# One 512-column first product for two token pairs, and a rewritten order of steps, in a gated-loop attention and feed-forward kernel

## The chip, the cores and the metric

One Trainium2 chip, one core of it. The time is the device time of one execution in microseconds, and the median of several executions is compared. TensorE (PE in the rows) does matrix products into PSUM, VectorE (DVE) and ScalarE (ACT) do elementwise work, GpSimd (POOL) and SyncE (SP) mostly issue DMA transfers.

## The reference

A gated linear attention with a complex decay for 4 batches, 8 heads, 768 steps and a head size of 48, then a feed-forward block with a silu:

```python
def _attn_ref(q, k, v, a_re, a_im):
    mag = np.sqrt(a_re * a_re + a_im * a_im)
    scale = np.minimum(mag, 0.999) / (mag + 1e-06)
    a_re_n, a_im_n = (a_re * scale, a_im * scale)
    for t in range(S):
        ar, ai = (a_re_n[:, :, t, :, None], a_im_n[:, :, t, :, None])
        new_re = ar * S_re - ai * S_im
        new_im = ar * S_im + ai * S_re
        kv = np.einsum('bhd,bhe->bhde', k[:, :, t], v[:, :, t])
        S_re, S_im = (new_re + kv, new_im)
        y[:, :, t] = np.einsum('bhd,bhde->bhe', q[:, :, t], S_re)

def _moe_ref(x, w_in, w_out):          # x: 3072 x 384, d_ff = 2048
    h = x @ w_in
    g = h * (1.0 / (1.0 + np.exp(-h)))
    return (g @ w_out).astype(np.float32)
```

## The kernel before

The 3072 tokens are 24 chunks n of 128; two chunks make a pair p, of which there are 12. Chunks 0 to 3 are the first of the four batches, chunk n carries on from chunk n - 4. For each chunk the attention runs in matrix form: gates and angles of a pair (steps G0 to Ga, ScalarE and VectorE), running sums of the angle and of the log decay by a triangular matmul (phase, L), rounding and sine (rd, turn, trig), decays (exp), decayed and rotated keys and queries (dk, dq, K, Q, or rk, rq), their transposes, scores (w) and their mask (m), the output (y), its copy into the pair's xT (x, and xd for the part of two heads that travels by DMA), and the state for the chunk four later (s, ss, sd, S).

The feed-forward part takes a pair's 256 tokens as moving operand of the first product, 256 hidden units at a time: step h:p.jp, jp from 0 to 7, fills one PSUM bank with two blocks of 128 units by 256 tokens. For pairs 2 to 11 the fp32 product is made of three products in fp32r: x and the weights are each split in forms, xH (head), xL (tail) and xD (difference) for x, the weights' head, `fine1` and `mixed1` on the other side (`hidden`, L749, and `sums`, L764). The forms of x are made by xh (ScalarE, L778), xt and xg (VectorE). Then silu (g:p.jp, ScalarE), the three forms of its result (gr on ScalarE, gb and gc on VectorE), and the second product r:p.jp (`result_of_parts`, L939), which adds 3 forms x 2 blocks of units x 2 output tiles to the pair's two PSUM tiles. After jp = 7 the tiles are copied out and stored (oc).

From pair 2 on, two neighbouring pairs make a quad; they share the loads of the weights' `fine` part and `diff` part from DRAM (lv, lw) and the `mixed` tile (vx), which are made under the quad's first pair (`lead`). The PSUM tiles are two banks for attention, two for h and four for the output. The buffers of xH, xL and xD are one for even and one for odd pairs; before pair 2 the same buffers serve the start of the attention.

The order of every engine's work is one list of 1899 steps written out by hand (L1079 to L1218). Each engine runs its own instructions in the order of that list, and so do the DMA queues: a step with g behind its number loads over GpSimd's queue, other loads and the weight blocks (F) go over SyncE's. H, J and R convert weight blocks, `warm:n` issues n matmuls without use, `hold` takes one weight buffer until GpSimd gets there. ScalarE loads a table of functions when a step needs a function of another set (`special`, L309).

Of the kernel before, what the change touches and what calls it, by code (L numbers as in the profile page):

```python
# [70 lines left out]
def kernel(  # L71
# [703 lines left out]

    def x_head(p):
        t = A[p]["xH"] = moe.tile([C, ND, T], F32R, tag=f"xH{p % 2}", name=f"xH{p}", bufs=1)
        nc.scalar.mul(t, A[p]["xT"], MORE * SPLIT / FINER)  # L778
# [616 lines left out]
```

## Time and profile before

| | us |
|---|---|
| median of 3 runs | 616.13 |
| lowest, highest | 613.35, 617.29 |
| the profiled execution | 616.33 |
| its span, first to last instruction | 614.5 |

The rows below are from the profiled execution; their times count from the start of the span. Matmuls overlap in the rows: the time of one runs from its start until its last result is in PSUM, so the distance of two starts, not the time of one, tells what a matmul costs in a sequence.

### The profile page before, as it was taken

How to read it: one execution, taken by the hardware profiler on the slowest of the kernel's cores; microseconds unless marked ns; L12 is line 12 of the kernel's file. 1: busy time of each engine (PE TensorE's matmuls, PEld its weight loads, DVE VectorE, ACT ScalarE, POOL GpSimd, SP SyncE). 2: the span in 40 equal slices, each digit the busy share in tenths (PEclk: the TensorE clock that was granted, in tenths of full speed). 3: DMA queues.
4: the chain of work that ended last, by engine and by line, in shares of the span. 5: the costliest groups of instructions: out<-in, count | busy, mean ns of one | idle time of the engine just before them, and what ended most of it. 6: DMA issues, size and time to landing. Idle time of an engine off the chain costs nothing. (4 is left out here: it accounts for less than half of the span.)

```text
span 614.5 us, 12718 instructions
## 1 busy us (share of the span) xinstructions
PE 584.0 (95%) x4404; PEld 538.2 (88%) x4404; DVE 495.9 (81%) x765; ACT 434.0 (71%) x689; POOL 222.4 (36%) x389
## 2 busy tenths in 40 slices
PE   3678999999998999999999999999999999999997
PEld 2457877777768999999999999999999999999996
DVE  5689989889988899888798989889989686566453
ACT  7789989799496798598797596897984742333222
POOL 6256343543631345533272553325640233000000
PEclk9879999999999999999999999999999999999999
DMA  9859698987778989768967768786768576664462
GB/s 180 201 136 190 184 195 189 203 160 205 202 234 244 218 163 238 161 157 186 212 159 186 154 156 225 180 187 149 177 156 255 146 186 155 203 201 136 160 201 80
DMA packets 167733, 112.30 MB, mean 183 GB/s; under 512 B 137725, under 2 KB 143425, under 8 KB 167665
## 3 DMA queue, kind: packets, MB, share of 16 engines
q1 hardware_dynamic: 151920, 89.69, 57.0%
q0 software_dynamic: 12288, 17.23, 14.0%
q10 hardware_dynamic: 3456, 4.52, 2.0%
q8 instruction: 36, 0.59, 0.4%
q14 instruction: 33, 0.26, 0.1%
HBM read 81.14 MB, written 11.47 MB: 151 GB/s over the span
## 5 line engine op out<-in xcount | busy, mean ns | idle before, releaser
L596 POOL DMA_DIRECT2D T<-sq x120 | 69.9, 590 | 67.3 <-PE h L768 24.0
L914 ACT ACTIVATE head<-g 128x512 fp32r<-128x512 f32 x75 | 47.4, 632 | 56.1 <-PE o L953 47.1
L312 ACT ACTIVATE g<-h 128x512 f32<-128x512 f32 x96 | 56.2, 593 | 40.5 <-PE h L768 34.4
L768 PE MATMUL h<-xL,fine 128*128 128x256 f32 x480 | 83.7, 283 | 0.8 <-DMA fine<-w_firsts 0.8
L768 PE MATMUL h<-xD,mixed 128*128 128x256 f32 x480 | 82.8, 280 | 1.0 <-DVE mixed L862 0.6
L306 ACT ACT_TABLE_LOAD x63 | 80.8, 1283 | 2.3 <-ACT ot L966 0.8
L858 DVE SCALAR_TENSOR_TENSOR tail<-g,head 128x512 fp32r<-128x512 f32 x75 | 51.5, 687 | 31.3 <-ACT head L914 21.6
L527 POOL DMA_DIRECT2D dec<-ends x48 | 31.3, 663 | 106.7 <-DMA ends<-eq 99.2
L768 PEld LDWEIGHTS h<-xD,mixed 128*128 128x128 f32 x480 | 68.5, 189 | 1.6 <-DVE mixed L862 1.0
L768 PEld LDWEIGHTS h<-xL,fine 128*128 128x128 f32 x480 | 68.3, 188 | 1.1 <-DMA fine<-w_firsts 1.1
L953 PE MATMUL o<-coarse,head 128*128 128x384 f32 x300 | 66.8, 344 | 0.0
L953 PE MATMUL o<-diff,gd 128*128 128x384 f32 x300 | 65.4, 339 | 0.7 <-DMA diff<-w_diffs 0.7
L768 PE MATMUL h<-xH,firsts 128*128 128x256 f32 x360 | 62.5, 282 | 0.0
L609 PE MATMUL a<-T 96*128 96x128 f32 x384 | 52.8, 285 | 3.9 <-ACT T L601 3.9
L953 PE MATMUL o<-fine,tail 128*128 128x384 f32 x260 | 55.6, 336 | 0.0
L609 PEld LDWEIGHTS a<-T 96*128 96x128 f32 x384 | 49.9, 198 | 6.5 <-ACT T L601 4.9
L953 PEld LDWEIGHTS o<-diff,gd 128*128 128x128 f32 x300 | 53.6, 188 | 1.5 <-DVE w L620 1.0
L862 DVE TENSOR_TENSOR gd<-tail,g 128x512 fp32r<-128x512 f32 x75 | 51.4, 686 | 4.2 <-PE o L953 0.2
L768 PEld LDWEIGHTS h<-xH,firsts 128*128 128x128 f32 x360 | 52.7, 188 | 0.5 <-issue 0.4
L953 PEld LDWEIGHTS o<-coarse,head 128*128 128x128 f32 x300 | 50.2, 188 | 1.5 <-issue 1.3
L728 POOL DMA_DIRECT2D S<-ssq x84 | 46.9, 607 | 12.8 <-DVE ssq L717 6.7
L953 PEld LDWEIGHTS o<-fine,tail 128*128 128x128 f32 x260 | 46.2, 188 | 0.0
(159 smaller groups left out, 1283.8 us busy)
## 6 DMA issues: line engine op xcount, KB each, us to landing
fine<-w_firsts SPq DMA_DIRECT2D x40, 384.0 KB
diff<-w_diffs SPq DMA_DIRECT2D x40, 384.0 KB
T<-sq SPq DMA_DIRECT2D x120, 64.0 KB
T<-sq POOLq DMA_DIRECT2D x120, 64.0 KB, 3.8
small<-in_moe_w_in_dram SPq DMA_DIRECT2D x16, 384.0 KB
raw<-in_moe_w_out_dram SPq DMA_DIRECT2D x16, 384.0 KB
small<-in_moe_w_out_dram SPq DMA_DIRECT2D x16, 384.0 KB
raw<-in_moe_w_in_dram SPq DMA_DIRECT2D x24, 192.0 KB
```

The costliest lines, as they stand in the source:

```text
L306: nc.scalar.preload_act_table_set(SETS[of][0])
L312: nc.scalar.activation(out=out, in_=in_, func=func, **kw)
L527: nc.gpsimd.dma_start(out=x["dec"][a * D:(a + 1) * D], in_=ends[n].rearrange("(h d) -> d h", d=D))
L596: (nc.gpsimd if a % 2 else nc.sync).dma_start(out=to[ts(b, Q), :, a], in_=X[n]["sq"][ts(a, Q), b].rearrange("p w h x -> p (w h) x"))
L609: nc.tensor.matmul(ps[:, h], lhsT=x["kT"][hh * HH + h], rhs=x["qT"][hh * HH + h], start=True, stop=True)
L728: (nc.gpsimd if g % 2 else nc.sync).dma_start(out=to[ts(b, Q), r, :, e], in_=sq[ts(g, Q), :, b, 0:e.stop - e.start])
L768: nc.tensor.matmul(ps[:, ji], lhsT=w(dc, ji), rhs=x[:, dc], start=(f == 0 and dc == 0), stop=(f == len(forms) - 1 and dc == ND - 1))
L858: nc.vector.scalar_tensor_tensor(out=dst, in0=whole, scalar=MORE / FINER, in1=head.bitcast(F32), op0=ALU.mult, op1=ALU.subtract)
L862: nc.vector.tensor_tensor(out=dst, in0=tail, in1=whole, op=ALU.subtract)
L914: nc.scalar.mul(g_form(p, jp, "head"), A[p]["g", jp], MORE * SPLIT / FINER)
L953: nc.tensor.matmul(to, lhsT=left[:, ji, ts(m, C)], rhs=right(ji), start=(first_ and ji == 0 and n == 0), stop=(last_ and ji == 1 and n == 2))
```

## The change

For the pairs 2 to 9 (`wide`), the four quads, a step h:p.jp computes one block of 128 units, block 2 jp + p % 2, for the 512 tokens of both pairs, as 9 matmuls of 512 columns in place of 18 of 256. So the two pairs' xH are the halves of one tile, and so are xL and xD (`quad_tile`), for all pairs; before pair 2 the halves of those tiles serve the start (`spare_form`). The second product of a step then has one block of units and the tokens of both pairs: 3 forms x 2 pairs x 2 output tiles, with the first and last step counted over the 16 steps of a quad. Pairs 0 and 1 (fp32) and 10 and 11 keep their products. The list of steps holds the same 1899 steps in another order from beginning to end.

```diff
@@ hidden(p, jp)
             fine, diff = (A[lead(p)][name, jp] for name in ("fine1", "mixed1"))
+            if wide(p):
+                forms = [(J[kind, lead(p)], w) for kind, w in
+                         (("xH", head_of(lead(p), jp)), ("xL", fine), ("xD", diff))]
+                for f, (x, w) in enumerate(forms):
+                    for dc in range(ND):
+                        nc.tensor.matmul(ps, lhsT=w[:, dc, ts(p % 2, C)], rhs=x[:, :, dc],
+                                         start=(f == 0 and dc == 0),
+                                         stop=(f == len(forms) - 1 and dc == ND - 1))
+                return
...
+    def wide(p):
+        return QUADS <= p < NP - 2
+
+    def quad_tile(key, i, dtype, name):
+        both = J.setdefault(key, None)
+        if both is None:
+            both = J[key] = moe.tile([C, 2, ND, T], dtype, tag=key[0], name=name, bufs=1)
+        return both[:, i]
+
+    def x_form(p, kind):
+        return quad_tile((kind, p - p % 2), p % 2, F32R, f"{kind}{p}")
+
+    def spare_form(kind, i, name):
+        return quad_tile((kind, -1), i, F32, name).rearrange("p c x -> p (c x)")
+
     def x_head(p):
-        t = A[p]["xH"] = moe.tile([C, ND, T], F32R, tag=f"xH{p % 2}", name=f"xH{p}", bufs=1)
+        t = A[p]["xH"] = x_form(p, "xH")
...
     def result(p, jp):
+        if wide(p):
+            result_of_quads(p, jp)
+            return
...
+    def result_of_quads(p, jp):
+        x, both = A[p], (lead(p), lead(p) + 1)
+        for q_ in both:
+            if "o" not in A[q_]:
+                A[q_]["o"] = o_tiles(q_, 2)
+        y = A[both[0]]
+        y["through"] = y.get("through", 0) + 1
+        first_, last_ = y["through"] == 1, y["through"] == NJ
+        forms = ((x["head", jp], W["coarse"][:, jp * 2 + p % 2]),
+                 (x["tail", jp], W["fine", jp][:, p % 2]),
+                 (x["gd", jp], y["diff", jp][:, p % 2]))
+        for n, (left, right) in enumerate(forms):
+            for i, q_ in enumerate(both):
+                for m in range(2):
+                    nc.tensor.matmul(A[q_]["o"][m].rearrange("p n c -> p (n c)"),
+                                     lhsT=left[:, i, ts(m, C)], rhs=right,
+                                     start=(first_ and n == 0), stop=(last_ and n == 2))
```

The order, at the start, and where the first quad (pairs 2 and 3) hands over to the second (4 and 5) and that to the third (6 and 7):

```diff
-                re:0 im:0 e0:0 re:1g e1:0 e2:0 q:0g e3:0 im:2g im:1 e4:0 e0:1 hold: e1:1 re:2g e6:0
-                e2:1 im:3g re:3g e5:0 k:0g F: v:0g e7:0 e4:1 e8:0 e6:1 F: L:0 e3:1 exp:0 e7:1 e8:1
-                at:0.0 warm:30 e5:1 F: dk:0 G0:1 k:1g an:0.0 dq:0 G5:1 phase:0 rd:0 R: turn:0
-                warm:34 at:0.1 sm:1 trig:0 L:1 an:0.1 H: rk:0.0 G1:1 rk:0.1 rq:0.0 phase:1 rd:1 H:
...
+                re:0 im:0 hold: e0:0 warm:34 re:1g e1:0 re:2g e2:0 e4:0 e0:1 e3:0 im:1 k:0g F: e5:0
+                e6:0 e1:1 im:2g warm:30 e7:0 L:0 e2:1 e4:1 e3:1 e8:0 e5:1 exp:0 re:3g e6:1 e7:1 H:
+                at:0.0 e8:1 an:0.0 at:0.1 an:0.1 warm:20 phase:0 im:3g G0:1 rd:0 dk:0 turn:0 F:
+                q:0g R: G8:1 q:1g v:0g R: ends:0 trig:0 G5:1 L:1 rk:0.0 sm:1 J: G1:1 dq:0 rq:0.0
+                exp:1 rk:0.1 s:0 F: H: rq:0.1 G7:1 lk:1 F: k:1g phase:1 dq:1 G2:1 rd:1 G4:1 sm:0 H:
+                H: v:1g lk:0 thirds:0 J: G3:1 last:0 L:2 R: R: G6:1 exp:2 t:0.0 F: turn:1 G9:1 dk:1
+                q:2g trig:1 T:0.0 S:0 t:0.2 T:0.2 L:3 re:4g Ga:1 k:2g t:0.1 ends:1 exp:3 F: t:0.3
+                rk:1.0 rq:1.1 rk:1.1 phase:2 rd:2 t:1.0 T:0.1 t:1.3 T:1.0 R: T:0.3 H: dq:2 w:0.0
...
-                gr:2.6 gb:2.6 gc:2.6 r:2.6 ul:13 xh:4 g:3.6 turn:13 w:11.1 g:2.7 xt:4 gr:3.6 xg:4
-                lw:2.7 gb:3.6 trig:13 tk:12 sd:10 G0:7 tq:12 h:3.7 g:3.7 w:11.0 v:12 G5:7 G1:7
-                gc:3.6 m:11.0 lv:4.0 r:3.6 m:11.1 gr:2.7 G7:7 td:12 y:11 x:11 gb:2.7 gc:2.7 r:2.7
-                xd:5 gr:3.7 G2:7 L:13 exp:13 vx:4.0 last:13 h:4.0 lv:4.1 gb:3.7 xh:5 w:12.1 gc:3.7
...
+                h:2.7 ul:13 h:3.7 lv:4.0 G0:7 turn:13 gb:2.6 K:12 g:3.7 gc:2.6 g:2.7 tk:12 w:11.0
+                tq:12 G5:7 m:11.0 r:2.6 xh:4 gr:3.6 G8:7 w:11.1 m:11.1 gb:3.6 y:11 td:12 gc:3.6
+                r:3.6 v:12 L:13 G1:7 x:11 xd:5 gr:2.7 xt:4 gb:2.7 gc:2.7 r:2.7 G2:7 w:12.0 q:13
+                gr:3.7 G7:7 q:15 xg:4 exp:13 vx:4.0 gb:3.7 gc:3.7 G3:7 lv:4.1 G6:7 sd:11 xh:5 xt:5
+                G9:7 w:12.1 r:3.7 oc:3.1 xg:5 Ga:7 m:12.0 h:4.0 carried:14 g:4.0 m:12.1 h:5.0 dk:13
+                im:16 carried:15 gr:4.0 vx:4.1 s:12 oc:2.1 g:5.0 oc:2.0 last:13 h:4.1 trig:13
+                lw:4.0 ends:13 h:5.1 v:13 ht:14 oc:3.0 lv:4.2 G4:7 k:15 gb:4.0 gc:4.0 g:4.1 dq:13
...
+                turn:17 G1:9 gr:4.6 Q:16 lw:4.6 h:4.7 xh:6 x:14 S:13 tk:16 G7:9 tq:16 w:15.0 G3:9
+                w:15.1 m:15.0 lw:4.7 m:15.1 gb:4.6 gc:4.6 v:16 g:4.7 G6:9 y:15 lv:6.0 x:15 r:4.6
+                gr:5.6 gb:5.6 G9:9 gc:5.6 r:5.6 gr:4.7 xt:6 G8:9 gb:4.7 L:17 gc:4.7 r:4.7 g:5.7
+                td:16 xd:7 k:17 xg:6 gr:5.7 gb:5.7 gc:5.7 w:16.0 vx:6.0 exp:17 lv:6.1 dk:17 r:5.7
+                xh:7 xt:7 w:16.1 G2:9 xg:7 v:17 sd:14 h:6.0 Ga:9 g:6.0 oc:5.0 oc:5.1 h:7.0 m:16.0
```

## Rows read from the trace of the kernel before

**Rows 1.** The page: span, and busy us (share of the span) xinstructions

```profile
span 614.5 us, 12718 instructions
PE 584.0 (95%) x4404; PEld 538.2 (88%) x4404; DVE 495.9 (81%) x765; ACT 434.0 (71%) x689; POOL 222.4 (36%) x389
```

**Rows 2.** Windows: stretch, its length, busy us of each engine, granted clock, DMA share

```profile
0.00:40.00 40.00, 19.61 (x127) 14.86 (x128) 26.45 (x50) 31.50 (x50) 20.35 (x40) 0.93 0.80 183
40.00:80.00 40.00, 37.60 (x303) 31.70 (x303) 36.66 (x70) 36.67 (x60) 19.04 (x28) 0.94 0.73 177
200.00:480.00 280.00, 279.31 (x2331) 272.54 (x2329) 246.65 (x366) 217.31 (x342) 117.94 (x213) 1.00 0.77 184
...
540.00:610.00 70.00, 70.00 (x488) 69.71 (x486) 37.22 (x61) 22.44 (x40) 0.00 (x0) 1.00 0.51 164
```

**Rows 3.** TensorE's waits: us in total, times, longest

```profile
PE L L462 <- DVE l L394: 10.6, 1, 10.6
...
PE h L768 <- DMA fine<-w_firsts: 0.8, 1, 0.8
...
PE h L768 <- DVE xD L862: 0.3, 1, 0.3
```

**Rows 4.** Groups by line of ScalarE: xcount | busy, mean ns | idle before, releasers

```profile
L306 ACT ACT_TABLE_LOAD x63 | 80.8, 1283 | 2.3 <-ACT ot L966 0.8 <-ACT ot L960 0.4
L312 ACT ACTIVATE g<-h 128x512 f32<-128x512 f32 x96 | 56.2, 593 | 40.5 <-PE h L768 34.4 <-DVE gd L862 3.4 <-PE h L761 1.5
L914 ACT ACTIVATE head<-g 128x512 fp32r<-128x512 f32 x75 | 47.4, 632 | 56.1 <-PE o L953 47.1 <-DVE w L620 3.5 <-issue 2.4
L312 ACT ACTIVATE mag<-mag 128x768 f32<-128x768 f32 x33 | 27.8, 842 | 0.9 <-ACT ot L966 0.4
...
L312 ACT ACTIVATE eq<-L 128x384 f32<-128x384 f32 x24 | 11.7, 487 | 2.6 <-PE L L462 1.5 <-PE L L465 1.0
...
L966 ACT COPY ot<-o 128x384 f32<-128x384 f32 x18 | 8.5, 474 | 6.3 <-DMA out_dram<-ot 2.9 <-PE o L953 2.5 <-ACT ot L966 0.9
```

**Rows 5.** Timeline of TensorE (start us, us, operation, xcount): beginnings of sequences

```profile
333.70 0.86 PE L953 MATMUL o<-coarse,head 128*128 128x384 f32 x4
...
335.79 0.52 PE L768 MATMUL h<-xH,firsts 128*128 128x256 f32 x3
...
340.07 0.52 PE L465 MATMUL phase<-th_parts,upto_r 128*128 128x384 f32 x2
```

**Rows 6.** Timelines of TensorE, ScalarE and VectorE where quad 2 ends

```profile
269.44 0.45 PE L639 MATMUL y<-w,v 128*64 128x128 f32 x4
...
271.04 0.44 PE L642 MATMUL y<-T,S 96*64 96x128 f32 x4
276.27 0.84 ACT L778 ACTIVATE xH<-xT 128x768 fp32r<-128x768 f32 x1
278.14 0.96 DVE L862 TENSOR_TENSOR xD<-xL,xT 128x768 fp32r<-128x768 f32 x1
```

**Rows 7.** Timelines of the start: VectorE, ScalarE, TensorE

```profile
18.90 0.56 DVE L540 TENSOR_TENSOR k<-k,L 128x384 f32<-128x384 f32 x1 [3.75 <-DMA k<-in_k_dram]
19.96 0.56 DVE L435 SCALAR_TENSOR_TENSOR th<-mag,re 128x384 f32<-128x384 f32 x1
15.41 0.52 ACT L312 ACTIVATE mag<-mag 128x384 f32<-128x384 f32 x1
17.01 0.84 ACT L312 ACTIVATE s<-re 128x768 f32<-128x768 f32 x1 [1.07 <-DMA re<-in_a_re_dram]
21.95 0.58 ACT L312 ACTIVATE turn<-phase,round_b 128x384 f32<-128x384 f32 x1 [2.64 <-PE phase L462]
43.76 1.37 PE L462 MATMUL phase<-th,upto_r 128*128 128x384 f32 x2
```

**Rows 8.** Timeline of TensorE: fp32 matmuls of pair 0 and what follows

```profile
66.19 2.76 PE L761 MATMUL h<-xT,w 128*128 128x256 f32 x12
68.79 1.06 PE L609 MATMUL a<-T 96*128 96x128 f32 x8
```

More of the change, by code (lines that the diff above doesn't have):

```diff
@@ L122 @@
     STREAM = 3
+    J = {}
     consts = ctx.enter_context(tc.tile_pool(name="consts", bufs=1))
@@ new lines @@
+                T:3.1 t:3.0 w:3.1 G9:2 T:3.0 im:7g m:2.1 s:3 m:3.1 g:0.1 H: w:3.0 F: S:3 Ga:2 L:4
+                J: R: m:3.0 thirds:2 H: J: h:0.2 y:2 exp:4 R: g:0.0 v:5g x:2 R: y:3 carried:4 H:
+                phase:4 F: J: H: J: x:3 rd:4 turn:4 re:6g g:0.2 trig:4 h:0.3 re:7g carried:5 R:
+                k:5g ends:4 dq:4 F: L:5 F: last:4 r:0.0 dk:4 H: Q:4 K:4 phase:5 k:6g g:0.3 J: tk:4
+                F: R: J: exp:5 G0:3 h:1.0 R: tq:4 rd:5 r:0.1 G5:3 H: G1:3 h:1.1 G2:3 ends:5 H: J:
+                G7:3 F: G3:3 turn:5 G8:3 s:4 H: r:0.2 td:4 G4:3 G6:3 F: S:4 R: R: J: dk:5 G9:3
@@ new lines @@
+                g:1.0 last:5 Ga:3 J: F: L:6 H: R: R: r:0.3 r:1.0 w:4.1 dq:5 F: carried:6 h:0.4
+                trig:5 J: K:5 Q:5 g:1.1 exp:6 g:0.4 H: sm:2 phase:6 rd:6 F: m:4.1 H: h:1.2 J: R:
+                carried:7 s:5 F: lk:2 H: H: H: im:8g re:8g R: im:9g R: h:1.3 turn:6 J: re:9g L:7
+                last:6 S:5 q:6g tk:5 g:1.2 dk:6 F: trig:6 phase:7 R: J: tq:5 J: F: ends:6 G0:4 J:
+                K:6 dq:6 Q:6 r:1.1 rd:7 G5:4 h:1.4 k:8 g:1.3 exp:7 h:1.5 F: R: H: R: H: J: td:5 H:
+                G1:4 k:7g R: J: J: turn:7 r:0.4 v:7g G7:4 G2:4 w:4.0 G8:4 vh:1 ends:7 r:1.2 m:4.0
@@ new lines @@
+                gr:2.0 lv:2.1 Ga:5 vx:2.1 h:2.1 h:3.1 carried:10 wk:1 gb:2.0 gc:2.0 v:9 of:0 K:9
+                lw:2.0 re:12 g:2.1 ss:8 ws:6 ht:10 carried:11 m:8.0 r:2.0 gr:3.0 ends:9 tk:9 s:9
+                ut:10 phase:10 hl:10 gb:3.0 lv:2.2 last:9 sm:3 gc:3.0 ul:10 ss:9 r:3.0 vx:2.2 dq:9
+                wk:6 re:13 L:10 rd:10 k:10 gr:2.1 lw:2.1 Q:9 ht:11 turn:10 g:3.1 gb:2.1 lv:2.3
+                gc:2.1 lk:3 h:3.2 exp:10 g:3.2 h:2.2 ut:11 tq:9 ends:10 r:2.1 gr:3.1 gb:3.1 gc:3.1
+                g:2.2 q:11 last:10 r:3.1 vx:2.3 phase:11 gr:2.2 w:8.1 dq:10 im:12 gb:2.2 S:7 gc:2.2
@@ new lines @@
+                ut:18 vx:6.2 g:7.1 r:6.0 phase:18 g:6.1 rd:18 q:18 h:7.2 hl:18 ss:16 lw:6.1
+                carried:19 lk:8 gr:6.1 ul:18 L:18 ht:19 S:15 re:20 gb:6.1 gc:6.1 k:18 turn:18 h:6.2
+                r:6.1 ut:19 Q:17 im:21 gr:7.0 exp:18 gb:7.0 lw:6.2 gc:7.0 k:19 phase:19 r:7.0
+                last:18 gr:7.1 ends:18 tk:17 trig:18 gb:7.1 re:21 rd:19 gc:7.1 tq:17 dq:18 g:7.2
+                hl:19 lv:6.3 g:6.2 q:20 turn:19 ul:19 r:7.1 vx:6.3 y:16 s:17 dk:18 h:7.3 gr:6.2
+                G0:10 gb:6.2 lv:6.4 G5:10 x:16 G8:10 Q:18 h:6.3 gc:6.2 g:6.3 K:18 r:6.2 gr:7.2
```

251 lines of the change are left out of this document (110 added, 141 removed).

## The prediction

> **What bounds the kernel now.** I read the busy shares first, then the same by stage, because the kernel has two halves with different limits. Over the span TensorE is busy 584.0 of 614.5 us [rows 1]. By stage [rows 2], the first 40 us leave TensorE idle for 20.4 us, although part of its busy time there is 84 matmuls without use (the list's warm steps); 40 to 80 us run at 37.6 of 40 us, with VectorE and ScalarE at 36.7 each, so that all three are full; from 200 us TensorE is busy 279.31 of 280, and at the end 70.00 of 70. VectorE is at 88% (246.65 of 280) and ScalarE at 78% in the 280 us. So from 40 us TensorE sets the time, and what ends earlier there ends earlier at the output, as long as nobody starves it. The list of TensorE's waits [rows 3] says the same: the longest, 10.6 us, lies in the start, and those of the loop of products are 0.8 us for a load and 0.3 us for xD.
>
> The profile's execution took 616.33 us, 1.83 us more than its span; the median of the three runs is 616.13, so the sum below is made on the span and 1.83 is put back.
>
> **Part 1: the first product of pairs 2 to 9.** A pair's step h:p.jp was 18 matmuls of 256 columns (two blocks of 128 units, three forms, three slices of the model dimension); 18 by 8 by 10 pairs are 1440. Now a step is 9 matmuls of 512 columns: one block of 128 units, the tokens of both pairs. Eight pairs by eight steps is 64 steps, so 576 matmuls and 576 weight loads go, and the columns streamed stay the same. What is saved is only what a matmul costs beside its columns. That I read from starts, since matmuls overlap: 36 matmuls of 256 columns start between 335.79 and 340.07, so 4.28 / 36 = 118.9 ns each; 12 of 384 columns between 333.70 and 335.79, 174.2 ns each [rows 5]. The granted clock is 1.00 here, the 2.4 GHz level [rows 2], so the columns take 106.7 and 160.0 ns, and 12.2 and 14.2 ns are left over.
>
> The trace has no 512-column matmul. Bounds: if nothing is left over, 213.3 ns; if time grows with the columns as at 256, 237.8 ns; as at 384, 232.3 ns. I take the nearest row's remainder as fixed: 213.3 + 14.2 = 227.5 ns. A step then goes from 18 x 118.9 = 2140 ns to 9 x 227.5 = 2048 ns: 92 ns, and 64 x 92 = **5.9 us** saved. The bounds give 64 x (2140 - 1920) = 14.1 us and nothing (18 x 118.9 is 9 x 237.8).
>
> A rule speaks against this part. The Trainium skill (TensorE: Matmul & The Clock Gate, section Back-to-back issue gap) has the gap of a warm matmul at its columns over 2.4 GHz plus about 2.5 ns. By it, 576 times 2.5 ns, only 1.4 us, would be saved, and the order would have to do the rest. The rows disagree with it: 12.2 and 14.2 ns are left over here, five times as much.
>
> **Part 2: the second product.** Its step was 12 matmuls of 384 columns and still is: 128 units, three forms, two pairs, two tiles each. Nothing is gained or lost there. What ScalarE and VectorE do to a step keeps its width (silu and head, 128x512, 593 and 632 ns [rows 4], and two operations on VectorE), and the loads of the weights' parts are the same.
>
> **Part 3: what a quad now needs at once.** h:4.0, which needed pair 4's xH, xL, xD, now needs both pairs', and r:4.0 adds to the four output tiles of the quad, so that the four copies of the quad before must be done. The tiles of the x forms come as one for both halves, so those of a new quad wait for the last first product of the old one, not of one pair. This happens three times (into quads 4, 6, 8), and similarly once into pair 10. At the first, the old order ran y:11 from 269.44 to 271.48, and the chain from there (copy out, the part by DMA, xH at 276.27, xL, xD to 279.10) took 7.6 us [rows 6]. In the new list TensorE has between y:11 and h:4.0 three second products (3 x 2.09), one L (two matmuls of 384 columns, 0.35) and two groups of scores (eight fp32 matmuls of 128 columns, 0.87 each, half of what [rows 8] has for 256), 8.4 us, and xD is wanted only after six further matmuls, 1.4 us: 9.8 against 7.6, a slack of 2.2. The tightest handover by its list is the one into quad 6. Counted from h:4.7, if ScalarE had run nothing ahead, its list up to xH of pair 7 holds four table loads (1.28), two silus (0.59), three heads (0.63), two xH (0.84), three activations of 768 columns (0.84), and six of 384 or fewer (at most 0.49): 15.3 us [rows 4, 6]. VectorE's xL and xD add 1.9: 17.2. TensorE has in that stretch four second products (8.4), four groups of scores (3.5), y:15 (2.0) and one L (0.35), 14.2 us, and the 1.4 us of the first six matmuls: 15.6, so 1.6 us late. ScalarE waits for TensorE more often than the reverse (47.1 us before its heads and 34.4 us before its silus, in the idle times of [rows 4]), so it does run ahead. I take 1.0 us for all handovers, between 0 and 3 x 1.6 = 4.8. The four copies (474 ns each [rows 4]) have four first products, 8.2 us, between r:3.7 and r:4.0, which hides them; without that cover they would cost 1.9 us at each handover.
>
> **Part 4: the order.** The list holds the same 1899 steps in another order. Following the functions' tables through both, ScalarE's table loads rise from 63 to 69, six at 1283 ns [rows 4], 7.7 us; one of the six comes early, before g:0.1, in the full stretch, and may cost its 1.3 us there (a part of rival (c)); the other five come where TensorE is the bound and ScalarE has 22% free, which hides them; were ScalarE full, they would be 6.4 us. I take nothing for all six.
>
> At the start the order matters. Before, VectorE sat at dk:0 until k had landed (18.90), with an:0.0 behind it, so th was written at 19.96 and the rounding behind phase:0 ran at 21.95 [rows 7], though the arctangent had been done at 15.93. Now k is loaded third on GpSimd's queue, not seventh, and dk:0 stands behind both angles: an:0.0 can run at 16 and phase:0 at about 17. But G0:1 stands ahead of the rounding on ScalarE, and waits for the last gate load (17.01 before); q:0 and q:1 have moved behind these loads and one weight block fewer is fetched early, while the first block's fetch now goes out at once. G0:1 is 2.5 us, so the rounding comes at about 19, **3.0 us** earlier. Bounds: 21.95 - 17.1 - 1.3 = 3.5 us, if G0:1 is not late; nothing, if it starts at 19.5. From there ScalarE's list is packed; phase:2, at 43.76 before, needs its work up to G9:1 (some 15 us, with two table loads) and would come near 39 to 40, with w:0.0 still to do behind it. The 34 and 30 warming matmuls stand ahead of L:0 and fit into its wait of 10.6 us.
>
> **Sum.** 614.5 - 5.9 - 3.0 + 1.0 = 606.6 us of span, and 606.6 + 1.83 = **608.4 us**.
>
> **The rivals.** (a) Beside a 512-column matmul nothing is left over, and the columns alone count: 614.5 - 14.1 - 3.0 + 1.0 + 1.83 = 600.2. For it: the rows show no fixed remainder. Against it: it grew from 256 to 384. (b) Only a little is fixed, and the rest grows with the columns. Twelve fp32 matmuls of 256 columns take 68.79 - 66.19 = 2.60 us, 216.7 ns each [rows 8], twice 106.7 and 3.3 over; were the fixed part 3.3 in the form of the change too, 64 x 9 x 3.3 = 1.9 us would be saved: 614.5 - 1.9 - 3.0 + 1.0 + 1.83 = 612.4. Against it: the remainder of 12.2 and 14.2 ns rose by 2 for 128 more columns, where in proportion it would have risen by 6. This is the case of the rule named above, whose 2.5 ns these fp32 rows nearly show. (c) The start's 3.0 us are lost between 40 and 80 us, where ScalarE and VectorE are at 92%: 614.5 - 5.9 + 1.0 + 1.83 = 611.4. For it: three full engines there, and a list written anew. (d) The handovers starve TensorE: the second pair's xH waits behind table loads and gates on ScalarE, and h:4.0, h:6.0 and h:8.0 stand still for it. At 3.0 us each (8.9 / 3) the gain is gone, from 5.0 us each ((8.9 + 6.2) / 3) the kernel is over 1% slower; at 6 us: 614.5 - 8.9 + 18 + 1.83 = 625.4. For it: both halves now come late or early together. Against it: 1.6 us is the most that I could count, and the measured chain leaves slack.
>
> **Chances.** The forecast 0.48, (a) 0.12, (b) 0.14, (c) 0.16, (d) 0.10. 1%, about what a measurement of this kernel can tell from no change, is 6.2 us: below 610.0 it is faster. The forecast's own spread (605 to 612) lies three quarters below that, 0.36; with (a) and a little of (c), 0.50 faster. Same: 0.12 of the forecast, 0.13 of (b), 0.13 of (c): 0.38. Slower: (d), and 0.02 of (b) and (c): 0.12. Range 601 to 618: it leaves out about 0.07 below and 0.11 above.
>
> **What would show it.** TensorE's matmuls fall from 4404 to 3828; nine first-product matmuls with 512 columns start within 2.05 us of each other (1.92 for (a), 2.12 for (b)). Phase:0 starts near 17 us and phase:2 near 40. TensorE's waits for xH, xL, xD or the output tiles stay under 1.5 us in all; over 9 us would be (d). The forecast is wrong if the start is no shorter, if TensorE's busy time after 200 us falls under 99% of the stretch, or if the table loads turn up in its waits.

## The result, and the profile after

The changed kernel takes 606.66 us (median of four runs, 605.07 to 607.66), the kernel before beside it 615.04 (613.35 to 617.29): ratio 0.9855, 95% interval 0.9818 to 0.9892, so 8.4 us less. Forecast was 608.4. The profiled execution of after took 605.07 us, the lowest of its four; that of before lay above its median. The two traces therefore differ by 614.5 - 603.4 = 11.1 us of span, and the sums below, made on traces, come to 11.1 and not to 8.4.

The page of the changed kernel: its span, and for each engine busy us, share and instructions.

```profile
span 603.4 us, 11507 instructions
...
PE 583.3 (97%) x3828; PEld 509.3 (84%) x3828; DVE 495.7 (82%) x765; ACT 441.2 (73%) x695; POOL 222.5 (37%) x389
```

TensorE has 3828 matmuls in place of 4404, but is busy for 583.3 us, hardly less than the 584.0 of [rows 1]. That figure alone would say that the products cost what they did. It does not: from the first product of the quads on TensorE needs 4.0 us less (below), and ahead of it the same number of matmuls keeps it busy for longer. In the first 40 us it is busy for 28.78 us, before for 19.61 [rows 2]; both kernels have 84 warming matmuls there, 12 us, but the changed one has more of the start's work there, and at a lower granted clock (0.79 against 0.93). Two rows of the kernel before, and one of the changed kernel where the clock is at the 1.2 GHz level:

```profile
32.65 2.35 PE L990 MATMUL idle<-upto_r 128*128 128x256 bf16 x20
34.83 1.48 PE L699 MATMUL s<-v,kr 128*96 128x48 f32 x16
...
22.77 1.52 PE L705 MATMUL s<-v,kr 128*96 128x48 f32 x8 [2.57 <-DVE kr L558]
```

Sixteen of these matmuls took 1.48 us before; now eight take 1.52. (The row of warming matmuls, idle<-upto_r, is needed further down.)

Windows of the changed kernel; the columns are those of [rows 2].

```profile
0.00:40.00 40.00, 28.78 (x148) 20.10 (x149) 31.25 (x61) 35.66 (x57) 21.52 (x40) 0.79 0.91 205
...
40.00:80.00 40.00, 36.97 (x303) 31.75 (x302) 38.54 (x71) 39.00 (x63) 21.31 (x33) 1.00 0.83 195
...
200.00:480.00 280.00, 279.54 (x1882) 251.95 (x1882) 243.25 (x360) 223.91 (x349) 117.47 (x212) 1.00 0.76 181
```

Read ScalarE, the fourth engine's column. In the first 80 us it did 35.66 + 39.00 = 74.7 us of work, against 31.50 + 36.67 = 68.2 before [rows 2]: it stood still for 5.3 us instead of 11.8. One table load of 1.28 us among this work is new, so 5.2 of the 6.5 us are work that came forward. From 200 us TensorE is as full as before (279.54 of 280), with 1882 matmuls in place of 2331 there.

TensorE's starts in the changed kernel: the first product of the first quad, where the loop ends one step and begins the next, and its last row; behind them the first and the last of these in the kernel before.

```profile
175.18 1.15 PE L766 MATMUL h<-xH,first 128*128 128x512 f32 x3
...
339.29 0.86 PE L766 MATMUL h<-xH,firsts 128*128 128x512 f32 x3
...
341.39 0.85 PE L766 MATMUL h<-xH,firsts 128*128 128x512 f32 x3
...
343.47 2.04 PE L613 MATMUL a<-T 96*128 96x128 f32 x16
...
598.39 0.52 PE L1004 MATMUL o<-diff,forms 128*128 128x384 f32 x2
```

```profile
182.28 0.82 PE L768 MATMUL h<-xH,first 128*128 128x256 f32 x3
...
609.52 0.52 PE L953 MATMUL o<-diff,forms 128*128 128x384 f32 x2
```

Two steps of nine matmuls take 343.47 - 339.29 = 4.18 us: 232.2 ns a matmul and 2.09 us a step. The quads' first product starts at 175.18 us; in the trace before it started at 182.28. TensorE's last row of matmuls starts at 598.39, before at 609.52. So the 11.1 us fall into 182.28 - 175.18 = 7.1 us ahead of that first product, and (609.52 - 182.28) - (598.39 - 175.18) = 427.2 - 423.2 = 4.0 us behind it.

The start of the changed kernel, of ScalarE, VectorE and TensorE, put in order of time.

```profile
16.70 0.84 ACT L313 ACTIVATE s<-re 128x768 f32<-128x768 f32 x1
...
16.93 0.56 DVE L436 SCALAR_TENSOR_TENSOR th<-mag,re 128x384 f32<-128x384 f32 x1
...
17.54 1.37 PE L463 MATMUL phase<-th,upto_r 128*128 128x384 f32 x2 [2.76 <-DVE th L436]
...
18.47 0.55 DVE L541 TENSOR_TENSOR k<-k,L 128x384 f32<-128x384 f32 x1
...
19.02 0.58 ACT L313 ACTIVATE turn<-phase,round_b 128x384 f32<-128x384 f32 x1
...
36.76 0.91 PE L463 MATMUL phase<-th,upto_r 128*128 128x384 f32 x2 [0.35 <-DVE th L436]
```

dk:0 (the line with k<-k,L) now comes behind both angles, at 18.47, and does not wait; the angle th is written at 16.93 (before 19.96 [rows 7]), phase:0 starts at 17.54, and the rounding behind it at 19.02 (before 21.95). Phase:2 starts at 36.76, before at 43.76. The load of re that opens G0:1 was no longer late: s<-re ran at 16.70.

TensorE's waits in the changed kernel: total us, times, longest.

```profile
PE s L705 <- DVE kr L558: 3.3, 2, 2.6
PE phase L463 <- DVE th L436: 3.1, 2, 2.8
...
PE L L463 <- DVE l L413: 1.6, 1, 1.6
...
PE o L986 <- ACT ot L1017: 0.5, 1, 0.5
PE h L766 <- DMA fine<-w_firsts: 0.4, 1, 0.4
...
PE h L766 <- DVE xD L892: 0.3, 1, 0.3
```

Of the last three lines only the output tiles, 0.5 us at 368 us, belong to a handover from one quad to the next; the waits for a load (0.4) and for xD (0.3) lie at 184 and 177 us, in the first quad's first steps. The first three lie in the start. The wait of 10.6 us for the first l [rows 3] is gone, as 64 warming matmuls stand ahead of that product; the 1.6 us is a later wait, for l of chunk 2 at 29.46.

### The profile page after: what moved, and what is told of

It reads as the page before. It is cut to its first block, busy times and chain, and to the rows that moved or that the text cites. A ratio compares the mean times of both kernels' runs of the same rounds, so it can differ in the third digit from the quotient of the medians.

```text
span 603.4 us, 11507 instructions
## 1 busy us (share of the span) xinstructions
PE 583.3 (97%) x3828; PEld 509.3 (84%) x3828; DVE 495.7 (82%) x765; ACT 441.2 (73%) x695; POOL 222.5 (37%) x389
## 5 line engine op out<-in xcount | busy, mean ns | idle before, releaser
L307 ACT ACT_TABLE_LOAD x69 | 88.5, 1283 | 2.3 <-ACT ot L1017 0.8
L600 POOL DMA_DIRECT2D T<-sq x120 | 70.1, 609 | 31.1 <-PE a L613 10.6
L986 PE MATMUL o<-coarse,head 128*128 128x384 f32 x256 | 57.1, 344 | 0.5 <-ACT ot L1017 0.5
L766 PE MATMUL h<-xL,fine 128*128 128x512 f32 x192 | 55.3, 396 | 0.4 <-DMA fine<-w_firsts 0.4
L766 PE MATMUL h<-xD,mixed 128*128 128x512 f32 x192 | 55.2, 396 | 0.4 <-DVE xD L892 0.3
L986 PE MATMUL o<-diff,gd 128*128 128x384 f32 x256 | 55.4, 337 | 0.0
L986 PEld LDWEIGHTS o<-diff,gd 128*128 128x128 f32 x256 | 45.5, 188 | 0.2 <-DVE gd L892 0.2
L776 PE MATMUL h<-xT,w 128*128 128x256 f32 x192 | 43.7, 381 | 1.6 <-ACT xT L689 1.6
L766 PEld LDWEIGHTS h<-xD,mixed 128*128 128x128 f32 x192 | 35.7, 188 | 10.1 <-DVE xD L892 1.2
L766 PEld LDWEIGHTS h<-xL,fine 128*128 128x128 f32 x192 | 36.0, 188 | 9.4 <-DMA fine<-w_firsts 0.8
L968 PE MATMUL o<-w,g 128*128 128x384 f32 x128 | 43.5, 488 | 0.0
L776 PEld LDWEIGHTS h<-xT,w 128*128 128x128 f32 x192 | 36.0, 190 | 7.9 <-ACT xT L689 1.8
```

Source lines behind the costliest of these rows:

```text
L307: nc.scalar.preload_act_table_set(SETS[of][0])
L600: (nc.gpsimd if a % 2 else nc.sync).dma_start(out=to[ts(b, Q), :, a], in_=X[n]["sq"][ts(a, Q), b].rearrange("p w h x -> p (w h) x"))
L766: nc.tensor.matmul(ps, lhsT=w[:, dc, ts(p % 2, C)], rhs=x[:, :, dc], start=(f == 0 and dc == 0), stop=(f == len(forms) - 1 and dc == ND - 1))
L776: nc.tensor.matmul(ps[:, ji], lhsT=of_first(w1, dc, jp * 2 + ji), rhs=A[p]["xT"][:, dc], start=(dc == 0), stop=(dc == ND - 1))
L968: nc.tensor.matmul(A[p]["o"][m].rearrange("p n c -> p (n c)"), lhsT=A[p]["g", jp][:, ji, ts(m, C)], rhs=w2[jp][:, ji], start=(j == 0), sto ...
L986: nc.tensor.matmul(A[q_]["o"][m].rearrange("p n c -> p (n c)"), lhsT=left[:, i, ts(m, C)], rhs=right, start=(first_ and n == 0), stop=(las ...
```

## The experiments

Each ratio is to the kernel before, run on the same chip, with its 95% interval. The medians of the kernel before on the three chips were 616.63 us (order alone, both hybrids, k early), 615.61 (changed kernel again, split, lengths, table loads) and 615.88 (k late, more warming).

### The order without the wide product

`wide` gives False for every pair, so the changed list drives the products of before, 18 matmuls of 256 columns a step.

```diff
     def wide(p):
-        return QUADS <= p < NP - 2
+        return False
```

> The changed kernel with the pairs 2 to 9 computed as before (18 first-product matmuls of 256 columns a step), in the new order. Theory (a step of 512-column matmuls is 48 ns shorter, 64 steps, the rest of the gain is the order): 3 us slower than the changed kernel, about 609.7 us, 5.4 us faster than before. Rival of the prediction's size (92 ns a step): 612.6. Rival that the order alone brings everything: 606.7.

Measured: 612.96 us (ten runs), ratio 0.9965 [0.9933, 0.9998]. So the order alone gives 2 us here by the ratio and 3.7 by the medians, and the wide product 6 to 7 on top of it: the theory's 609.7 missed, and the time is that of the rival with the prediction's size (612.6). The trace, of an execution of 616.72 us, shows why this is no clean price of the product. TensorE's rows at the third step of the first quad (h:2.1), its window there (columns of [rows 2]) and its waits for the load:

```profile
186.26 1.01 PE L783 MATMUL h<-xL,fine 128*128 128x256 f32 x3 [1.64 <-DMA fine<-w_firsts]
187.35 1.01 PE L783 MATMUL h<-xD,mixed 128*128 128x256 f32 x3
188.16 0.84 PE L783 MATMUL h<-xH,lent 128*128 128x256 f32 x3
188.79 0.84 PE L783 MATMUL h<-xL,fine 128*128 128x256 f32 x3
```

```profile
182.00:194.00 12.00, 10.14 (x64) 9.33 (x63) 7.12 (x10) 4.40 (x8) 3.01 (x5) 0.72 0.62 167
```

```profile
PE h L783 <- DMA fine<-w_firsts: 2.0, 2, 1.6
```

The step's first product comes before its weight part has landed, TensorE stands for 1.64 us, and behind the wait each three matmuls take 1.09, 0.81 and 0.63 us from start to start, where 3 x 0.119 = 0.36 is their price in the loop; the granted clock of the window is 0.72 of the 2.4 GHz level. In the changed kernel the same load costs 0.4 us and no clock, in its second trace less. The narrow product doesn't make this wait: with 512-column products it is 0.15 us with more warming, 1.25 with more table loads and 1.34 with k late (all below). Two of these traces show the low clock behind it, this one and the last; the one with 1.25 us doesn't. What sets its length was not tried. The median of ten runs is what the price above rests on.

### The same order, each matmul split in two

The product is split again, but now with everything else of the changed kernel kept: the tiles of both pairs, the second product for one block of units, the order.

```diff
-                for f, (x, w) in enumerate(forms):
+                for i in range(2):
+                    for f, (x, w) in enumerate(forms):
...
-                        nc.tensor.matmul(ps, lhsT=w[:, dc, ts(p % 2, C)], rhs=x[:, :, dc],
+                            nc.tensor.matmul(ps[:, i], lhsT=w[:, dc, ts(p % 2, C)], rhs=x[:, i, dc],
```

> The changed kernel with every 512-column first-product matmul split into two of 256 columns with the same weights, loaded twice (18 a step again); order, tiles and waits stay those of the changed kernel, so the number of matmuls alone is undone. Theory from the first trace (232 ns for 512 columns, 118.9 for 256): 64 x 48 ns, 3.1 us slower than the changed kernel. The prediction's size (227.5 ns): 5.9 us slower. Rival that fewer matmuls bring nothing and the order everything: 0.

Measured: 612.46 us (ten runs, 611.11 to 616.18), ratio 0.9954 [0.9925, 0.9983]; the changed kernel, run again on the same chip, took 606.53 (605.01 to 608.11), ratio 0.9849 [0.9811, 0.9888]:

> The changed kernel itself, timed on the same chip as the experiments below and with a second trace. Expected from the first timing (0.9855 of before): 607 to 609 us here; its progress at the copies of chunk 7's output some 6 to 7 us ahead of before, at the end 9 to 11.

The changed kernel's second trace agrees with its first: a span of 603.3 us and the first product of the quads at 175.32. It came a little below the 607 to 609 us that were expected; the copy for chunk 7 is 7 us ahead of the kernel before, and the end 11.

So 576 matmuls more cost 5.9 us, just the term of the prediction and nearly twice the theory's 3.1. But the trace doesn't give them the size of that term. From the first product of the quads on, the time spent in first products is 177.2 us against 172.8 in the changed kernel, 4.4 more. By the prices of the loop the matmuls are 64 steps of 18 x 118.9 - 9 x 232.2 = 50 ns, or 3.2 us; the other 1.2 us is TensorE standing between them. What is left of the difference is 0.8 us elsewhere behind the start and 0.6 ahead of it, no more than such runs scatter. Its waits:

```profile
PE o L987 <- ACT ot L1018: 1.0, 1, 1.0
PE h L767 <- DVE mixed L893: 1.1, 3, 0.5
```

The `mixed` tile is not among the waits of the changed kernel and holds up three steps here, by 1.1 us; the output tiles cost 1.0 instead of 0.5. That the waits belong to the split rather than to this one execution was not tried.

### What a matmul costs by its length, alone

Behind the end of the changed kernel, with all other engines still, come series of 36 matmuls each, in fp32r as in the kernel: 512 columns from one run of memory and from both halves of a quad's x tile, 384, 256, and 512 and 256 with weights for 64 units.

```diff
+        for name, cols, rhs in (("c512", C, flat_[:, 0]), ("s512", C, two[:, :, 0]),
+                                ("c384", C, flat_[:, 0, 0:384]), ("c256", C, flat_[:, 0, 0:256]),
+                                ("h512", 64, flat_[:, 0]), ("h256", 64, flat_[:, 0, 0:256])):
...
+            for _ in range(36):
+                nc.tensor.matmul(to[0:cols], lhsT=left[:, 0:cols], rhs=rhs, start=True, stop=True)
```

> The changed kernel with six series of 36 fp32r matmuls behind its last step, while the other engines stand still; nothing reads their results. 512 columns in one strip, in two strips of 256 as in the change, 384, 256, and 512 and 256 columns with weights of 64 columns in place of 128. If the time beside the columns belongs to fp32r matmuls as such: 232, 232, 174, 118 ns. If it comes from other engines' reads and writes in the loop: 213 to 216, 160 to 163, 107 to 109. If two strips cost: the first series is faster than the second. If it is the weights' load showing through: the last two series are nearer to 213 and 107.

Timeline of TensorE behind the end; a row can hold two series (x72), the six take their turn in the order above.

```profile
600.70 8.56 PE L1286 MATMUL c<-firsts,coarse 128*128 128x512 f32 x36
...
609.10 8.56 PE L1286 MATMUL s<-xH,coarse 128*128 128x512 f32 x36
...
617.49 10.60 PE L1286 MATMUL c<-firsts,coarse 128*128 128x384 f32 x72
...
627.93 12.71 PE L1286 MATMUL h<-firsts,coarse 128*64 128x512 f32 x72
```

Starts 8.40 us apart are 233.3 ns for a 512-column matmul from one run of memory, and 8.39 us are 233.1 from two. By the starts within the joined rows 384 columns take 173.3 ns, 256 take 116.7; with weights for 64 units 512 take 230.9 and 256 take 117.7. It is one execution. Two matmuls of 256 columns, 233.4 ns, cost what one of 512 does. Beside the columns at 2.4 GHz (213.3, 160.0, 106.7) are left 20.0, 13.3 and 10.0 ns. So the remainder is no overhead of one matmul: it is 8 to 9% of the columns, it is there with every other engine still, and neither the second run of memory nor the width of the weights makes it. The bf16 matmuls don't have it: the twenty warming matmuls of 256 columns shown above start (34.83 - 32.65) / 20 = 109.0 ns apart, 2.3 over the columns, at the 2.4 GHz level. In the kernel's loop the 512-column matmul costs the same (232.2) but the 256-column one 118.9 [rows 5], 2.2 ns more than alone. The loop's price for many short matmuls is nearly all that the change gets back from TensorE's matmuls.

### The changed kernel from the old start, and the old kernel from the new one

Two hybrids. In the first, the steps ahead of h:0.0 in the changed kernel's list stand in the order of the kernel before; in the second, the steps ahead of h:0.0 in the list of before stand in the new order. Nothing else is changed. The first lines of the edit in the first hybrid (the second has the signs the other way round):

```diff
-                re:0 im:0 hold: e0:0 warm:34 re:1g e1:0 re:2g e2:0 e4:0 e0:1 e3:0 im:1 k:0g F: e5:0
-                e6:0 e1:1 im:2g warm:30 e7:0 L:0 e2:1 e4:1 e3:1 e8:0 e5:1 exp:0 re:3g e6:1 e7:1 H:
...
+                re:0 im:0 e0:0 re:1g e1:0 e2:0 q:0g e3:0 im:2g im:1 e4:0 e0:1 hold: e1:1 re:2g e6:0
+                e2:1 im:3g re:3g e5:0 k:0g F: v:0g e7:0 e4:1 e8:0 e6:1 F: L:0 e3:1 exp:0 e7:1 e8:1
...
```

> The changed kernel with the steps that stand ahead of its first h:0.0 put back into the order that they had before; the rest, and the 512-column products, stay. Theory (the start's 4 to 5 us reach the end): 611 us. Rival (the start's gain is lost behind it, and the later order brings the rest): 606.7.

> The kernel before with only the steps ahead of its first h:0.0 in the order of the changed kernel. Theory (4 to 5 us from the start, carried to the end): 610.5 us. Rival (ScalarE and VectorE are full from 40 to 80 us and give it back): 615.

Measured: the changed kernel from the old start 612.84 us, ratio 0.9945 [0.9913, 0.9976]; the old kernel from the new start 615.4, ratio 0.9982 [0.9953, 1.001], no difference. The two halves of the order don't add: the new start is worth 5.5 to 6 us under the new list (0.9945 against 0.9855 and 0.9849) and 1 under the old one. Where the old kernel loses it again is read from ScalarE's roundings (turn<-phase) for chunks 2 and 4, in the kernel before, in the second hybrid and in the changed kernel:

```profile
45.17 0.58 ACT L312 ACTIVATE turn<-phase,round_b 128x384 f32<-128x384 f32 x1 [0.29 <-PE phase L462]
...
80.25 0.58 ACT L312 ACTIVATE turn<-phase,round_b 128x384 f32<-128x384 f32 x1 [1.38 <-PE phase L462]
```

```profile
38.93 0.58 ACT L312 ACTIVATE turn<-phase,round_b 128x384 f32<-128x384 f32 x1
...
78.25 0.58 ACT L312 ACTIVATE turn<-phase,round_b 128x384 f32<-128x384 f32 x1 [1.48 <-PE phase L462]
```

```profile
38.26 0.59 ACT L313 ACTIVATE turn<-phase,round_b 128x384 f32<-128x384 f32 x1
...
74.85 0.58 ACT L313 ACTIVATE turn<-phase,round_b 128x384 f32<-128x384 f32 x1 [0.38 <-PE phase L463]
```

In the hybrid chunk 2 is 6.2 us ahead of the kernel before, chunk 4 only 2.0. In the changed kernel the two are 6.9 and 5.4 us ahead. The hybrid's window:

```profile
40.00:80.00 40.00, 36.30 (x302) 31.77 (x301) 33.98 (x63) 35.05 (x58) 21.07 (x29) 0.96 0.72 168
```

ScalarE's work from 40 to 80 us is 35.05 us here against 39.00 in the changed kernel: between the early steps, in the new order, and the old list behind them it stands still again. The first hybrid loses at its seam too: its copy of chunk 2's output (x:2) runs at 81.99, where the kernel before has it at 72.08 and the changed one at 72.98, and its first product of the quads comes at 184.45, later than in the kernel before (182.28). Its trace is of an execution of 616.48 us, 3.6 above its median. So the 6 us hold a loss at the seam and are an upper figure for the start, not its price. What the start brings is taken apart by smaller edits.

### The load of k, forward in the old list and back in the new one

In the kernel before, the load of k:0 moves to the third place of GpSimd's queue and dk:0 behind the rounding; in the changed kernel both go back.

```diff
@@ the kernel before @@
-                re:0 im:0 e0:0 re:1g e1:0 e2:0 q:0g e3:0 im:2g im:1 e4:0 e0:1 hold: e1:1 re:2g e6:0
+                re:0 im:0 e0:0 re:1g e1:0 e2:0 q:0g e3:0 k:0g im:2g im:1 e4:0 e0:1 hold: e1:1 re:2g
...
-                at:0.0 warm:30 e5:1 F: dk:0 G0:1 k:1g an:0.0 dq:0 G5:1 phase:0 rd:0 R: turn:0
+                at:0.0 warm:30 e5:1 F: G0:1 k:1g an:0.0 dq:0 G5:1 phase:0 rd:0 dk:0 R: turn:0
@@ the changed kernel @@
-                re:0 im:0 hold: e0:0 warm:34 re:1g e1:0 re:2g e2:0 e4:0 e0:1 e3:0 im:1 k:0g F: e5:0
+                re:0 im:0 hold: e0:0 warm:34 re:1g e1:0 re:2g e2:0 e4:0 e0:1 e3:0 im:1 F: e5:0 e6:0
...
-                at:0.0 e8:1 an:0.0 at:0.1 an:0.1 warm:20 phase:0 im:3g G0:1 rd:0 dk:0 turn:0 F:
+                at:0.0 e8:1 im:3g k:0g dk:0 an:0.0 at:0.1 an:0.1 warm:20 phase:0 G0:1 rd:0 turn:0
```

> The kernel before with two steps moved: the load of k:0 third on GpSimd's queue, not seventh, and the product dk:0 behind the rounding of phase:0. It tests the prediction's step that VectorE's stand at dk:0 cost 3 us. Theory: the first rounding comes at 19 us, not 21.95, and 3 us reach the end: 612 us. Rival: the rounding comes earlier and the rest of the start takes it back: 615.

> The changed kernel with the step at dk:0 undone: the load of k:0 stands behind the last gate load on GpSimd's queue (sixth, not third), and dk:0 ahead of an:0.0 on VectorE as before. It is the counterpart of e4. Theory (e4 gave 3.1 us of the start's gain by this step): the first rounding comes near 21 us, not 19, and the kernel takes about 3 us more than the changed one, 609.6. Rival (in the new order ScalarE's list sets the pace and the step is worth nothing): 606.6.

Measured: the kernel before with k early 613.48 us, ratio 0.9951 [0.9927, 0.9975], 3.1 us less than the kernel before beside it. The changed kernel with k late 609.64, ratio 0.9883 [0.9835, 0.9931], 2.9 us more than the 606.79 of another variant on the same chip that has the changed kernel's time (more warming, below), 3.1 more than the changed kernel run again on another chip (606.53); by the two ratios it is 0.34 points, 2.1 us. From both sides this step is worth 2 to 3 us. In the first of the two the rounding came at 20.22, later than the theory's 19, but from chunk 2's rounding on (41.26) it is 3.9 us ahead. The first of the two, ScalarE's first rounding and the windows (columns of [rows 2]):

```profile
20.22 0.56 ACT L312 ACTIVATE turn<-phase,round_b 128x384 f32<-128x384 f32 x1
```

```profile
0.00:40.00 40.00, 21.29 (x137) 15.61 (x138) 28.88 (x56) 33.78 (x54) 21.25 (x41) 0.98 0.86 197
...
40.00:80.00 40.00, 37.90 (x309) 32.20 (x309) 36.86 (x69) 37.71 (x63) 20.11 (x30) 0.98 0.80 184
```

And the second, VectorE at dk:0 and ScalarE at the first rounding:

```profile
18.26 0.56 DVE L541 TENSOR_TENSOR k<-k,L 128x384 f32<-128x384 f32 x1 [3.16 <-DMA k<-in_k_dram]
```

```profile
21.68 0.58 ACT L313 ACTIVATE turn<-phase,round_b 128x384 f32<-128x384 f32 x1 [2.66 <-PE phase L463]
```

VectorE stands 3.16 us for k, th is late, and ScalarE waits 2.66 us for phase:0; the rounding moves from 19.02 to 21.68, and the quads' first product from 175.18 to 177.45. That is 2.3 us; the rest by which this trace is longer (608.1 us of span) comes behind it, where the load that was named above is late, with the low clock behind it (columns of [rows 2]):

```profile
186.97 1.18 PE L766 MATMUL h<-xL,fine 128*128 128x512 f32 x3 [1.34 <-DMA fine<-w_firsts]
```

```profile
182.00:194.00 12.00, 10.61 (x55) 7.96 (x54) 9.34 (x13) 5.68 (x10) 3.01 (x5) 0.86 0.70 192
```

In the kernel before, k alone left ScalarE idle for 80 - 33.78 - 37.71 = 8.5 us of the first 80, between the 11.8 of before and the 5.3 of the changed kernel. The k step is a third to nearly half of the 7.1 us that the start gained. Beside the rest stand the further 3.2 us that ScalarE doesn't stand still, 1.3 of them the new table load; which of the many moved steps does that was not taken apart.

### More warming in the start

The changed kernel's clock is at the 1.2 GHz level for a long stretch of the start: 0.57 granted from 16 to 36 us. Nineteen more warming matmuls are to keep it up.

```diff
-                q:0g R: G8:1 q:1g v:0g R: ends:0 trig:0 G5:1 L:1 rk:0.0 sm:1 J: G1:1 dq:0 rq:0.0
-                exp:1 rk:0.1 s:0 F: H: rq:0.1 G7:1 lk:1 F: k:1g phase:1 dq:1 G2:1 rd:1 G4:1 sm:0 H:
+                q:0g R: G8:1 q:1g v:0g R: ends:0 trig:0 G5:1 L:1 warm:12 rk:0.0 sm:1 J: G1:1 dq:0
+                rq:0.0 exp:1 rk:0.1 s:0 F: H: rq:0.1 G7:1 lk:1 F: k:1g phase:1 warm:7 dq:1 G2:1
```

> The changed kernel with 19 more matmuls without use in TensorE's idle time, 12 behind L:1 and 7 behind phase:1. In the changed kernel's trace the granted clock is 0.5 for 17.1 us, from 17.9 us on. Theory (ScalarE sets the pace of the start, TensorE's half clock is not on the path): within 1 us of the changed kernel, 606.6. Rival (the half clock delays the start's products): up to 2 us faster, and then it beats both kernels; if the added matmuls stand in the way, slower.

Measured: 606.79 us, ratio 0.9846 [0.9795, 0.9897], the time of the changed kernel. The window 16 to 36 us in the changed kernel, and in this one:

```profile
16.00:36.00 20.00, 12.80 (x40) 7.83 (x41) 18.69 (x34) 19.58 (x31) 8.73 (x13) 0.57 0.90 234
```

```profile
16.00:36.00 20.00, 12.17 (x59) 7.88 (x60) 18.63 (x34) 19.24 (x30) 8.86 (x13) 0.83 0.89 230
```

The clock did rise, from 0.57 to 0.83, and nothing came of it that four runs can show: ScalarE is at work for 19.58 and 19.24 of the 20 us and sets the pace, and TensorE, busy for 12.80, has time for its matmuls at the 1.2 GHz level. The interval is wide, some 3 us to either side, but the rival's 2 us are not seen against the changed kernel's 606.53 and 606.66.

### Nine more table loads

In the changed kernel the list asks for silu's table directly ahead of twelve silus, g:4.1 to g:4.6 and g:6.1 to g:6.6. Three of these loads take the place of one that the list had anyway, so there are nine more, 78 in place of 69, at 1283 ns each. The first of the twelve:

```diff
-                lw:4.0 ends:13 h:5.1 v:13 ht:14 oc:3.0 lv:4.2 G4:7 k:15 gb:4.0 gc:4.0 g:4.1 dq:13
+                lw:4.0 ends:13 h:5.1 v:13 ht:14 oc:3.0 lv:4.2 G4:7 k:15 gb:4.0 gc:4.0 table:silu g:4.1 dq:13
```

> The changed kernel with nine more table loads of ScalarE (78 for 69), each directly ahead of a silu of the second or third quad, 9 x 1.28 = 11.5 us of ScalarE's time. Theory (TensorE is the bound there, ScalarE has room; six more loads in the new order cost nothing): at most 1 us slower than the changed kernel. Rival (the silu is on the path from the first to the second product): up to 11.5 us slower.

Measured: 609.89 us (five runs, 608.71 to 612.39), ratio 0.9896 [0.9854, 0.9938], 3.4 us above the changed kernel beside it (606.53) for 11.5 us of added work. The theory's 1 us missed. The two intervals overlap, but the lowest of its five runs lies above the highest of the changed kernel's four. The window from 200 us on and a wait of TensorE that the changed kernel doesn't have:

```profile
200.00:480.00 280.00, 277.99 (x1846) 248.11 (x1846) 239.48 (x354) 232.69 (x353) 118.76 (x213) 1.00 0.77 180
```

```profile
PE h L766 <- ACT g L313: 0.8, 1, 0.8
```

ScalarE rises to 232.69 of 280 us and TensorE falls to 277.99 (279.54 in the changed kernel). Set beside the changed kernel's second trace, matmul by matmul, this one is 0.15 us behind at the first product of the quads (175.47 against 175.32) and 4.6 at the end (602.99 against 598.35, TensorE's last row). Of that, 1.1 us are the late load at 184.90, ahead of every added table load; 3.3 us come between 283 and 395 us, among the added loads (279 to 414 us), not quite half of them as waits that the profile lists. Behind 395 us nothing is added. So table loads under a full TensorE are not free at any place: where each stands directly ahead of a silu that TensorE will soon want, they cost some 30% of themselves, by this trace (3.3 of 11.5 us) as by the medians (3.4).

## Why the prediction was right, and where it was not

**The time** came within 1.7 us of the forecast, but not term by term, and that it came so near is partly luck: the products gave 2.9 us less than their term, the start 4.1 and the handovers 2.2 more. On the pair of traces that leaves 11.1 us against 7.9; by the medians it was 8.4, and 9.1 on the second chip. The prices of the experiments don't add up to it either: undoing the wide product costs 5.9 us, undoing the start 5.5 to 6, since what is left then waits at other places.

| | predicted | by the traces | |
|---|---|---|---|
| first products | -5.9 | -3.0 | 175.8 to 172.8 us, from the first product of the quads on |
| start | -3.0 | -7.1 | first product of the quads 182.28 to 175.18 |
| handovers, other idle time behind the start | +1.0 | -1.2 | TensorE idle 2.5 to 1.3 us |
| rest | 0 | +0.2 | |
| span | -7.9 | -11.1 | medians: -8.4 |

**Part 1, the product.** The failed step is "I take the nearest row's remainder as fixed: 213.3 + 14.2 = 227.5 ns". The matmul takes 232.2 ns, which is the bound that the same paragraph worked out for time growing with the columns as at 384 (232.3). A step takes 2.09 us, between the 2.05 of the forecast and the 2.12 of (b). Two lengths were there to tell a fixed part from a proportional one, and they told little: the 256-column row is 118.9 in the loop but 116.7 alone, so that it carries 2.2 ns of its own, which hid how nearly the rest is in proportion. The run with lengths shows it: 10.0, 13.3 and 20.0 ns over 256, 384 and 512 columns. So rival (b) had the mechanism right; its size (1.9 us) was too small by 1.1, the forecast's (5.9) too large by 2.9. (The twelve rows from which (b) has its 3.3 ns are six matmuls of the program, two rows to each, so that it is a remainder per row.) The rule of the Trainium skill (TensorE: Matmul & The Clock Gate, section Back-to-back issue gap), columns over 2.4 GHz plus about 2.5 ns, doesn't fit these fp32r matmuls: 20 ns are left over at 512 columns, not 2.5. It does fit the bf16 warming matmuls of the same traces, 109.0 ns for 256 columns, where the estimate by it is 109.2. A fixed part for fp32r the series alone don't show (two matmuls of 256 columns 233.4 ns, one of 512 233.3); the 2.2 ns are there in the loop only. Rival (a), 14.1 us, is out. The split kernel's 5.9 us look like a confirmation of the term and are none: 3.2 of them are matmuls.

**Part 2, the second product.** Nothing gained or lost, as said: it is in the rest of 0.2 us.

**Part 3, the handovers.** The cost of 1.0 us didn't come. Between quads only the output tiles are waited for, 0.5 us once; that ScalarE "does run ahead" was the right reading, and the count that assumed ScalarE had run nothing ahead gave the bound, not the case. Rival (d) is out. TensorE stands still less than before, 1.3 against 2.5 us.

**Part 4, the order.** That k's load held up the start was right, and so was its price: the rounding came at 19.02 (about 19 predicted), and the step is worth 3.1 us in the old list and 2 to 3 in the new one. Phase:0 at 17.54 (near 17 predicted). The step that failed is that the start's gain ends with this rounding, 3.0 us carried forward from it. "From there ScalarE's list is packed" is true of the new list, 19.58 of 20 us from 16 to 36; the old one was not packed in the same stretch, 15.43 of 20 (columns of [rows 2]):

```profile
16.00:36.00 20.00, 13.24 (x96) 10.22 (x94) 14.73 (x27) 15.43 (x24) 6.79 (x11) 0.91 0.79 193
```

So phase:2 came at 36.76, not at 39 to 40, and the rounding behind it at 38.26 against 45.17, a lead of 6.9 us where 3 had been carried forward; chunk 4's rounding has 5.4 and the quads' first product 7.1, and what makes the difference between these two was not taken apart. The windows of before had the room in plain sight: ScalarE busy 31.50 of 40 and 36.67 of 40 ("all three are full"), 11.8 us [rows 2], of which the new list uses 6.5. Rival (c), the start's gain lost between 40 and 80 us, is what happens to the old list from the new start (615.4), and not what happens in the changed kernel. That the further 3 to 4 us come from ScalarE standing still less fits its windows, in all but one of these traces:

| | ScalarE idle in the first 80 us | first product of the quads | ahead of before |
|---|---|---|---|
| before | 11.8 | 182.28 | |
| before, new start | 10.2 | 179.94 | 2.3 |
| before, k early | 8.5 | 178.23 | 4.1 |
| changed, k late | 7.9 | 177.45 | 4.8 |
| changed, more warming | 6.2 | 175.93 | 6.4 |
| changed | 5.3 | 175.18 | 7.1 |
| changed, old start | 11.6 | 184.45 | -2.2 |

That it is their cause is argued from them, not shown by a run that changes that alone: a kernel that is ahead for any reason has also done more of ScalarE's work by 80 us.

**The table loads.** Six more cost nothing that can be seen: no wait of TensorE names them. What the one in the start costs there, where ScalarE sets the pace, was not tried. That loads can cost nothing under a full TensorE, whatever their place, would have been wrong, as the nine extra loads show.

The range (601 to 618) had its spread from the bounds of the product. The start had a bound of 3.5 us, and gained 7.1 on the traces: it was that bound, not the product's, that was too narrow.

No version faster than the changed kernel was found. The one that was aimed at the start, with more warming, takes the same time.

## What to carry to other kernels

Halving the matmuls at the same columns pays some 5 ns for each one that goes here (3.0 us for 576), not the whole remainder over the columns; a second and a third length, measured alone, tell a fixed part from a proportional one, and two lengths from a running loop don't. In a stretch in which no engine is full over the whole of it, count the idle time of the one that is nearest to full: a single wait can be much less than what a new order wins there (3.0 us counted, 7.1 won, 11.8 idle). An order is worth what its whole list makes of it: under the old list 4.2 of the new start's 6.2 us were lost within 40 us. A load that comes late in one trace should be looked for in the others before it is put down to an edit.

## What the runs showed of the hardware

- An fp32r matmul takes 116.7, 173.3 and 233.3 ns for 256, 384 and 512 columns with every other engine still and the clock at the 2.4 GHz level, 8 to 9% more than its columns, whether the moving operand is one run of memory or two (233.3, 233.1). Half as many weight columns change little (117.7, 230.9). A bf16 matmul of 256 columns takes 109.0 ns, 2% more than its columns.
- TensorE at a granted clock of 0.57 over 20 us cost nothing that these runs show while ScalarE was busy for 19.58 of these 20 us; with the clock at 0.83 the time was the same, 606.79 against 606.53 us.
- Waits of 1.64 and 1.34 us in the first quad were followed by matmuls at a lower clock (granted 0.72 and 0.86 over 12 us around them) in two traces, a wait of 1.25 us at the same place in a third was not. The changed kernel's wait of 0.5 us in a handover has none of it: its granted clock from 200 to 480 us is 1.00.
- Nine table loads of 1283 ns cost 3.3 of their 11.5 us, each directly ahead of a silu, in a stretch in which ScalarE was busy for 83% of the time.
